# Attention and FFN kernel on one core: first q and k loads on one queue, the first GpSimd load behind the spin, and another order of the first 340 operations

## Chip, cores and metric

The kernel runs on one core of a Trainium2 chip. The metric is the device time of one execution in microseconds; before the change the median of three runs is 364.25 us (363.78 to 365.21).

## What is computed

Batch B=8, H=12 heads, sequence S=448, head size D=64. Attention without softmax: the scores are scaled, cut at zero, squared, and multiplied with v. Its result, 3584 rows of 768, goes through an FFN with exact GELU. Inputs and output are float32.

```
scores = scale * np.matmul(q, k.transpose(0, 1, 3, 2))    # scale = 1/sqrt(64)
attn = np.maximum(scores, 0.0) ** 2 / S
x = np.matmul(attn, v)              # then heads side by side: (3584, 768)
h = x @ w_in                        # 768 -> 2048
g = 0.5 * h * (1.0 + erf(h * inv_sqrt2))
return g @ w_out                    # 2048 -> 768
```

## The kernel before

The work goes batch by batch, and within a batch in three groups of four heads. For one group, k and q are brought into the layout in which the contraction (D) lies along partitions; TensorE makes scores in steps (`add_steps`, L819: four matmuls, two heads at a time, one block of keys), each into one of three PSUM banks "w"; ACT or DVE cuts them at zero and scales them (relu, L831 on ACT, L833 on DVE); DVE squares them (L841); TensorE multiplies with v (`add_av`, L881); ACT or DVE copies the result as `xT` (the copies of L566 on DVE and L568 on ACT). The FFN works on `xT`: matmuls with w_in (L940), GELU on ACT (L950), then w_out; later batches use a form with sums of operands (L1092, L1281). FFN matmuls of one batch are mixed with attention of later ones.

For batches 0 and 1 the change of layout is done on TensorE, with an identity matrix `ident` as the second operand: k in `add_tk` (L676, L680), q in `add_tq` (L708, L715), into one of two PSUM buffers "f", from which DVE or ACT copies them to `kT` and `qT`. For later batches the DMA queue of SyncE (SP) transposes.

Loads that turn float32 into bfloat16 on the way are issued by GpSimd (POOL): k (L605), q (L514), v (L623), w_in (L529 to L531), w_out (L535). At most eight are under way: a later one waits for the landing of the one eight ahead of it. Only the first group's k and the first half of its q take another way, at the start: they are loaded as float32 into `q32` and `k32` by SP and ACT (L1439 to L1442), k in a first part of four key blocks (256 KB) and a rest of three (192 KB), q's half being 224 KB; ACT casts q to `nq` and the rest of k to `nk` (L568), DVE casts the first part of k (L566). The second half of that group's q (112 KB in bfloat16's columns 128 of 256 a row) comes through GpSimd.

While the first loads are on their way, TensorE runs ten matmuls of 512 columns on a tile of zeros (L1461, the spin). `ident` is set to zero by DVE (L1445), and GpSimd puts the ones on its diagonal (affine_select, L1448).

The order is written out by hand: `ORDER` is a string of 1468 words, each an engine's letter (P TensorE, A ACT, D DVE, G GpSimd, S SyncE) with the number of an operation, and the scheduler emits the operations in that order. Each engine works through its own queue in order; an instruction that waits holds up all behind it on its engine. In the table P27 is the transposing of the second half of the first group's q (eight transposes), G7 its load; G0 and G1 are the loads of the second group's k and q; D13, A10 and A16 the casts of the first k part, the first q half and the rest of k; G1468 is the affine_select. The scheduler's numbers for when the first loads land are used to estimate times and don't change an order that is written out.

Of the kernel before, what the change touches and what calls it, by code (L numbers as in the profile page):

```python
# [12 lines left out]
B, H, S, D = 8, 12, 448, 64  # L13
KC = 112
NC = S // KC
HC = NC // 2
HS = S // 2
KB = 64
NK = S // KB
# [22 lines left out]
NB = 512  # L42
# [45 lines left out]
SPIN = 10  # L88
# [8 lines left out]
A58 A102 D91 P129 P143 D94 D100 D103 P158 A144 A159 P104 A105 A106 G132 P146 D130 D147 D128 S213
P229 P170 P182 D183 G9 A230 P155 A171 D154 A156 P227 G114 P140 A141 D160 P194 P164 D165 A195 A228
P237 P149 P173 G131 P200 G134 P239 A238 P241 D145 A150 A201 A174 D148 D157 A240 P176 A177 D151 D142
D172 P161 D184 A162 A242 D166 P179 P167 P235 P233 D175 D178 D163 D180 P197 P206 G118 A168 A236 D169  # L100
A198 D181 A234 P185 D207 P203 A186 P188 P231 A187 A232 P243 D214 G221 P247 A244 S212 A248 D202 D204
P249 A250 P245 D189 A246 P257 P272 D199 D205 P191 P269 D192 A258 A273 A270 G117 P255 A256 D190 G138
P251 P266 D196 D193 S215 P275 A276 D208 S216 D267 A252 P209 A210 P281 P284 A211 P356 P340 A282 G133
D217 D285 P290 P305 P308 D291 D292 A357 P342 G137 G260 A341 A309 P344 G259 G136 D283 D306 A343 A345
P253 P299 P293 P278 D268 D286 D279 D280 D271 A254 P350 A351 P352 A353 P358 A359 S219 D220 P346 A347
D300 D301 D277 P362 A363 P366 P364 P302 D294 S218 D274 D295 P317 D303 P287 A318 A367 P329 P296 A365
A288 D310 A330 D304 D307 D289 D297 P360 A361 P354 A355 G222 P370 G223 G225 G261 P326 S389 D390 P314
A315 P332 D333 A327 P372 P323 S388 P320 G262 A321 G264 G224 A371 D380 D298 P311 P439 S392 D324 D328
D322 D381 P430 P368 D383 A373 D384 A312 D334 D313 D316 A369 P348 A349 P338 A431 A339 P377 D382 A378
D385 A440 P411 S395 A412 G139 P445 D387 G226 A446 D325 D441 D407 G399 D386 P436 D331 D408 P433 P374  # L110
A375 A437 A434 P415 G263 G403 D393 D409 S391 P413 P457 P460 A461 S379 D319 D414 P335 P442 D458 P451
A336 A416 A452 P417 P419 D459 A443 A337 S394 D432 D396 D447 D418 D410 P454 P463 D420 P427 A428 P421
P423 P475 G265 D435 D553 D438 A455 A464 D429 P466 D444 G398 P448 D424 A476 D467 D422 G400 D456 G405
P478 P484 P521 G404 G397 G402 A485 D479 D462 D468 D477 A449 P525 D465 D453 A522 S532 A450 P469 P481
D533 A526 P487 A488 A470 P511 A482 S531 P517 P493 D471 P490 S538 P472 D494 D495 D483 S535 A491 A512
G540 D473 G401 A518 D474 P606 P594 P529 A607 A595 P519 A530 P597 P591 P603 A520 P527 D551 D552 D489
A604 D480 D605 A528 G545 P501 A502 P513 A514 D592 D608 D598 S534 P505 A506 G542 P507 P600 D492 D593
P609 D486 P496 A610 D536 A508 A497 D601 G406 A498 P627 P630 D631 P523 A628 D602 A524 S537 S539 P615
P618 P633 P503 P509 D632 A619 G548 D611 A634 A504 D635 P515 D629 A510 D596 P499 P621 D599 A616 S376
A500 A622 P624 G541 D625 P612 A516 A613 S696 D620 P657 D614 D617 D626 P645 A658 S702 G550 P555 A646  # L120
A556 G544 D554 S426 S695 P557 P559 D697 S425 D623 P757 S699 G710 P639 P636 A758 D640 G547 P648 D558
A560 P760 D637 A761 P561 A638 P563 D641 D562 G708 D700 G705 D659 P654 A649 D650 G706 P772 P651 A773
D564 D571 A655 P565 A652 D566 D573 D572 P567 D568 P766 P754 P642 A643 A767 D656 G546 G549 S698 G709
P575 D653 D644 P577 P769 D774 D768 D647 S701 A576 A755 P778 A779 D770 D762 P660 P763 G712 P790 A764
A661 A791 P579 D578 S569 P581 D756 P787 P793 D771 D574 A580 A662 P796 A794 A797 D582 D765 D780 D792
A788 P583 S703 D759 D584 D789 P585 P808 G543 G707 S827 P802 A803 P775 P784 S829 G842 D809 P781 D586
P587 P669 S826 D795 D828 A782 D783 G837 A776 A777 D798 A785 D714 A670 P805 S830 P814 A815 D786 D806
S833 P799 P811 D810 D588 P817 S831 S570 D800 D801 D804 P667 A818 P671 A812 A668 P870 A871 D807 P867
P873 D816 D874 A868 P677 A672 P876 P820 P864 D819 A678 P691 A692 A877 P689 G711 P673 D875 D872 D821
D715 G838 S832 P891 D813 A865 D822 D892 G840 G713 P894 P823 A690 P879 D824 A895 A674 D896 P900 A880  # L130
P665 A825 D834 P663 G843 G839 D866 A901 G835 G836 G704 P882 P888 A666 D869 A664 P903 A889 A883 P683
S937 S940 A684 D893 P687 P693 P927 D717 D878 A904 S942 P897 D881 D884 A928 P885 P906 D898 A688 A694
S943 D907 P921 P679 S941 S590 A680 P685 S939 D899 G841 D905 A922 D938 P681 A686 D944 S936 P718 D902
A682 D908 S589 D716 P675 A719 D890 D929 P722 A676 D923 A886 A887 P915 P912 P1000 A916 D913 P720
A1001 D917 P964 D914 P909 A965 D721 D1002 A723 P958 D966 P924 A910 G945 P724 A959 D925 A911 D960
P952 P976 D725 P930 A953 P726 D977 A931 D926 P918 P946 D932 A919 P728 D727 A947 D734 P979 D920 P933
A980 D729 D735 P955 D948 P949 A934 P730 A956 D950 A935 D957 P961 P994 D951 P1009 A962 P738 D731 A995
D963 S733 D954 P740 A1010 D739 S732 D736 P742 D741 D737 D996 P997 A743 P988 P967 D998 A989 D1011
P985 P1006 A968 D999 P744 A986 D1007 A969 D981 P1012 P973 P970 A1013 D745 P746 D974 A971 D1008 P1003
P982 A1004 D747 P748 D1014 A983 D1005 P750 D749 D984 S752 D972 P848 D975 D987 P1015 A849 D978 D990  # L140
D1018 P991 A1016 A1017 D1026 P852 A992 D1019 A993 D1027 P1030 D1021 P1049 A1031 P1051 D1028 A1050
P1144 D1052 P1068 A1145 D844 P1034 A1069 D751 P1125 A1035 D1022 P1055 A1126 P1148 D845 P1053 D1056
A1149 P1072 D1029 A1054 P1106 A1073 D1025 P1087 A1107 D1023 P1089 A1088 P1110 D1090 P1091 A1111 D846
P1093 A1092 D1020 P850 D1094 D847 P1061 D851 P1099 D1024 A853 P1127 P1032 D1062 P1095 D1128 A1063
P1108 D1033 D1096 P856 D1109 A1098 D1100 P1036 D1242 A1101 P1131 D1037 P854 D1132 D1243 P1137 D855
P1042 D1138 P1163 D857 A1139 P1038 D1043 A1164 P860 D1039 A1044 D1244 A1041 P1102 D861 P1133 D1245
P1129 D1134 P1045 A1130 D1103 P1167 A1136 D1046 A1105 P1165 A1168 P1070 A1048 D1166 P858 P1057 A1040
D859 P1140 A1047 D1071 S862 A1135 P1169 D1058 A1097 P1146 A1104 D1141 S753 A1059 P1064 D1170 A1142
A1143 P1112 D1147 A1060 S863 P1074 D1065 D1113 P1314 A1066 A1067 D1075 P1076 A1315 P1118 D1077 P1080
D1119 A1078 P1150 A1079 D1081 A1120 P1152 D1151 A1082 P1171 D1153 P1156 D1172 A1155 P1175 A1154  # L150
D1157 A1174 P1178 A1173 D1176 A1158 P1318 D1179 A1177 P1114 A1180 D1182 P1159 A1181 D1184 P1186
D1183 D1115 P1263 A1187 D1185 P1083 A1116 D1160 A1264 P1188 A1117 D1084 A1162 A1161 A1085 P1190
A1086 D1189 P1316 A1191 P1192 D1317 P1331 D1193 P1121 A1332 P1194 D1122 A1123 A1124 P1333 D1195
P1265 D1202 P1198 D1204 D1203 P1267 D1334 P1196 D1199 D1205 D1266 P1320 D1197 P1335 D1321 S1200
P1206 S1201 P1208 A1207 P1210 D1209 P1212 A1211 P1337 D1213 P1214 D1224 D1338 P1325 D1215 P1216
D1222 D1326 D1223 P1342 D1217 P1365 D1343 P1218 S1220 A1366 P1226 A1268 D1219 A1327 D1225 S1221
A1344 P1367 D1227 A1336 P1269 A1319 D1368 P1280 D1270 P1228 A1281 P1284 D1229 P1369 A1285 P1322
A1370 P1282 D1323 P1230 D1283 P1328 A1231 P1286 D1329 P1297 D1287 P1299 A1298 P1291 D1300 P1274
D1292 P1232 D1275 A1293 A1276 P1246 D1233 P1303 A1247 P1236 D1304 P1350 D1237 P1371 P1308 P1234
D1309 A1310 P1250 D1372 P1288 D1235 A1251 P1348 S1240 D1289 P1238 P1301 A1324 D1239 P1271 A1330  # L160
S1241 P1294 A1349 D1272 A1302 P1376 D1351 A1290 P1352 D1295 A1273 P1354 D1377 A1353 P1248 A1296
# [1491 lines left out]
```

## Time and profile before

| What | us |
|---|---|
| median of three runs | 364.25 |
| the profiled execution's own time | 364.45 |
| its span, first to last instruction | 362.7 |
| first scores (L819) start | 6.65 |
| first relu (L831) starts | 7.08 |
| first FFN matmul (L940) starts | 27.00 |

The profile shows one execution, in which times are counted from the start of its span. PE is TensorE's matmuls, PEld its loading of the stationary operand, which lies beside them; DVE is VectorE, ACT is ScalarE, POOL is GpSimd, SP is SyncE. A row of the timeline has the start, the length from first start to last end of a run of like instructions, the engine, the line, what is written and read with shapes, the count, and in brackets how long the engine had been idle and what released it. The rows themselves are shown where they are used, below.

### The profile page before, as it was taken

To read this page: it belongs to the slowest core of one execution; us is meant where nothing else is said; L and a number is where in the kernel's file an instruction comes from. 1 tells how busy PE (TensorE), PEld (TensorE's weight loads), DVE (VectorE), ACT (ScalarE), POOL (GpSimd) and SP (SyncE) were. 2 spreads that over 40 slices of the span, in tenths; PEclk is the share of its full clock that TensorE was granted. 3 is DMA by queue.
4 is the path that set the end of the run, shared out by engine and by line. 5 is a ranking of instruction groups with operands and counts; after the bars stand their busy time and mean duration, and the time that the engine had idled before them with its cause. 6 is when DMAs were issued, how large, how long until landed. Compare 5 with 4: busy or idle time off the path is not lost.

```text
span 362.7 us, 7632 instructions
## 1 busy us (share of the span) xinstructions
PE 353.4 (97%) x3099; PEld 189.9 (52%) x3099; DVE 296.4 (82%) x497; ACT 211.3 (58%) x354; POOL 67.1 (19%) x102
## 2 busy tenths in 40 slices
PE   8799999999999999999999999999999999999995
PEld 4464544555544555554455555555555555555663
DVE  3999788869999878999979999998966655786552
ACT  5999665546678685777958864625740333662110
POOL 8566174110902161070000000000000000000000
PEclk9999999999999999999999999999999999999999
DMA  9999999999999999999951511000301210302223
GB/s 172 201 202 201 184 175 194 173 197 207 160 188 152 228 203 146 220 168 202 164 133 11 95 61 45 3 0 19 114 0 53 78 45 2 87 2 87 88 89 88
DMA packets 72083, 43.83 MB, mean 121 GB/s; under 512 B 36336, under 2 KB 68720, under 8 KB 72048
## 3 DMA queue, kind: packets, MB, share of 16 engines
q0 software_dynamic: 32032, 22.47, 43.7%
q1 hardware_dynamic: 39120, 20.03, 29.8%
q10 hardware_dynamic: 896, 0.85, 0.7%
q8 instruction: 24, 0.39, 0.4%
q14 instruction: 11, 0.09, 0.1%
HBM read 45.61 MB, written 11.01 MB: 156 GB/s over the span
## 4 chain that ended last, share of the span: by engine, by line
PE 87%; DVE 5%; ACT 4%; issue 1%; DMA 1%; DVEq 0%
PE pso L1281 30%; PE psh L940 20%; PE pb L1092 18%; PE ps L819 8%; PE pav L881 7%; ACT a_sq L831 4%; PE pso L1388 3%; DVE a_sq L841 2%; DVE osb L1315 1%; DMA q<-in_q_dram 1%; DVE a_sq L833 1%; DVE qT L566 1%; ACT xT L568 0%; DVE s_sb L1260 0%; PE tp L715 0%
## 5 line engine op out<-in xcount | busy, mean ns | idle before, releaser
L831 ACT ACTIVATE a_sq<-ps 128x896 bf16<-128x896 f32 x122 | 107.1, 923 | 28.7 <-PE ps L819 27.0
L841 DVE TENSOR_TENSOR a_sq<-a_sq 128x896 bf16<-128x896 bf16 x169 | 96.8, 617 | 2.2 <-ACT a_sq L831 1.8
L940 PE MATMUL psh<-xT,win_sb 128*128 128x448 bf16 x384 | 77.1, 353 | 0.0
L833 DVE TENSOR_SCALAR a_sq<-ps 128x896 bf16<-128x896 f32 (+1 forms) x47 | 50.6, 1078 | 13.1 <-PE ps L819 12.8
L1281 PEld LDWEIGHTS <-s_sb 128*128 128x128 bf16 x424 | 40.4, 98 | 29.7 <-issue 3.5
L940 PEld LDWEIGHTS <-win_sb 128*128 128x128 bf16 x384 | 35.6, 98 | 38.0 <-issue 7.4
L1123 DVE TENSOR_TENSOR part<-pb,part 128x448 f32<-128x448 f32 x80 | 46.5, 620 | 9.0 <-PE pb L1092 6.2
L819 PE MATMUL ps<-qT,kT 64*64 64x448 bf16 (+1 forms) x700 | 48.2, 350 | 2.5 <-ACT a_sq L831 2.0
L950 ACT ACTIVATE h_sb<-psh 128x448 bf16<-128x448 f32 x64 | 34.4, 548 | 19.2 <-PE psh L940 19.2
L1315 DVE TENSOR_TENSOR osb<-pso,p_sb 128x384 f32<-128x384 f32 x39 | 21.7, 555 | 23.6 <-PE pso L1281 18.1
L1281 PEld LDWEIGHTS <-h_sb 128*128 128x128 bf16 x296 | 28.2, 98 | 21.5 <-issue 3.0
L1281 PE MATMUL pso<-t_sb,s_sb 128*128 128x384 bf16 x208 | 38.1, 326 | 0.0
L1144 ACT ACTIVATE h_sb<-part 128x448 bf16<-128x448 f32 (+1 forms) x48 | 24.5, 537 | 22.8 <-DVE part L1123 22.7
L1281 PE MATMUL pso<-wout_sb,s_sb 128*128 128x384 bf16 (+1 forms) x208 | 37.7, 324 | 0.0
L881 PE MATMUL pav<-a_sq,v_sb 64*64 64x448 bf16 (+1 forms) x700 | 36.0, 342 | 0.8 <-ACT a_sq L831 0.8
L1281 PE MATMUL pso<-wout_sb,h_sb 128*128 128x384 bf16 x192 | 35.2, 326 | 0.0
L819 PEld LDWEIGHTS <-kT 64*64 64x64 bf16 x700 | 18.4, 105 | 25.9 <-issue 19.1
L1092 PEld LDWEIGHTS <-win_sb 128*128 128x128 bf16 x192 | 18.8, 98 | 16.7
L881 PEld LDWEIGHTS <-v_sb 64*64 64x64 bf16 x700 | 20.6, 107 | 12.5 <-issue 2.1
L1092 PE MATMUL pb<-xs,ws 128*128 128x448 bf16 x96 | 21.9, 352 | 0.0
L1092 PE MATMUL pb<-xT,win_sb 128*128 128x448 bf16 x96 | 21.8, 352 | 0.0
L1092 PE MATMUL pb<-xs,win_sb 128*128 128x448 bf16 x96 | 21.8, 352 | 0.0
(71 smaller groups left out, 310.7 us busy)
## 6 DMA issues: line engine op xcount, KB each, us to landing
nk<-in_k_dram POOLq DMA_DIRECT2D x23, 224.0 KB, 8.5
nq<-in_q_dram POOLq DMA_DIRECT2D x23, 224.0 KB, 9.2
v_sb<-in_v_dram POOLq DMA_DIRECT2D x4, 672.0 KB, 9.7
out_dram<-osb SPq DMA_DIRECT2D x7, 336.0 KB, 3.3
v_sb<-in_v_dram POOLq DMA_DIRECT2D x10, 224.0 KB, 7.5
out_dram<-osb SPq DMA_DIRECT2D x7, 288.0 KB, 3.4
out_dram<-osb SPq DMA_DIRECT2D x8, 240.0 KB, 2.8
win_sb<-in_moe_w_in_dram POOLq DMA_DIRECT2D x8, 192.0 KB, 9.5
```

What stands on the lines that cost most here:

```text
L819: nc.tensor.matmul(ps[64 * j : 64 * j + 64, e, x * w : x * w + w], kT[r, g, i * 128 + 64 * j : i * 128 + 64 * j + 64], moving, start=True, ...
L831: A.activation(ar, ps, AF.Relu, scale=c_att)
L833: V.tensor_scalar(ar, ps, c_att, 0.0, op0=mybir.AluOpType.mult, op1=mybir.AluOpType.max,)
L841: V.tensor_mul(box["a2"][:, :, :used], ar, ar)
L881: nc.tensor.matmul(pav[0][o2 : o2 + 64, e, :w], get_v()[r, 2 * v_slot(b, g) + e, bass.ts(i, D)], box["a2"][r, y, o : o + w], start=(i == 0 ...
L940: nc.tensor.matmul(ph[:, x * n : x * n + n], win_sb[:, kd, bass.ts(m + x, 128)], xT[b][:, kd, c], start=(kd == 0), stop=(kd == KD - 1),)
L950: A.activation(h_ring()[:, m : m + nm, o + c.start : o + c.stop], box[0][:, :S].rearrange("p (x n) -> p x n", x=nm), AF.Gelu,)
L1092: nc.tensor.matmul(ps[name][:, :S], w[:, k, bass.ts(mm, 128)], right()[:, k], start=first and k == 0, stop=k == K1 - 1, skip_group_check=n ...
L1123: V.tensor_add(get(to), ps[name][:, :S], get(other))
L1144: A.activation(to(), src()[:, n0:n1], AF.Gelu)
L1281: nc.tensor.matmul(box[bank][:, n0:n1], left()[:, kf], right()[:, kf, n0:n1], start=bool(need) and kf == 0, stop=kf == K2 - 1, skip_group_ ...
L1315: V.tensor_add(out()[:, n0:n1], box[bank][:, n0:n1], other()[:, n0:n1])
```

## The change

It has five parts. The two loads of k move from ACT's DMA queue to SP's, behind q's. The spin becomes seven matmuls of 512 columns with one of 256 ahead and one behind, the first of which writes the second half of the bank. DVE copies a column of that second half into `ident`, and sets `ident` to zero only after that, so that GpSimd's affine_select has to wait for both. In `ORDER` that affine_select comes first and G7 ahead of G0 and G1, and some 340 further words are in another order (the table's rest, from P372 on, is the same but for the place of one load). The scheduler's landing times are other numbers.

```diff
-SPIN = 10
+SPIN = 7
 ORDER = """
-D13 G0 A10 G1 G7 G4 A16 G108 G1468 P11 D12 P14 D15 P17 P29 P32 D18 P38 D39 P19 P21 A30 D20 P35
...
+G1468 D13 G7 G0 A10 G1 G4 A16 G108 P11 G2 P14 D12 A15 G3 P27 P17 G111 A28 P32 D18 A33 G107 P53 P44
...
     first = slice(0, K_CUT * D)
-    nc.scalar.dma_start(k32[:, :, first], kv_view(k, 0, 0, 1)[:, :, first])
     nc.sync.dma_start(q32, q_view(0, 0, 1, 0, HC))
+    nc.sync.dma_start(k32[:, :, first], kv_view(k, 0, 0, 1)[:, :, first])
     rest = slice(K_CUT * D, NK * D)
-    nc.scalar.dma_start(k32[:, :, rest], kv_view(k, 0, 0, 1)[:, :, rest])
+    nc.sync.dma_start(k32[:, :, rest], kv_view(k, 0, 0, 1)[:, :, rest])
     zero = const.tile([128, 128], BF16, tag="zero", name="zero")
     V.memset(zero, 0.0)
-    V.memset(ident, 0.0)
...
     spin = banks.take("spin")
-    for _ in range(SPIN):
-        wide = zero[:, :1].to_broadcast([128, NB])
-        nc.tensor.matmul(spin[:, 0], zero, wide, start=True, stop=True)
+    for n, c in enumerate((NB // 2,) + (NB,) * SPIN + (NB // 2,)):
+        wide = zero[:, :1].to_broadcast([128, c])
+        nc.tensor.matmul(spin[:, int(n == 0), :c], zero, wide, start=True, stop=True)
+    V.tensor_copy(ident[:, :1], spin[:, 1, :1])
+    V.memset(ident, 0.0)
     banks.give(spin)
...
-    o = early("ACT", lambda: by_head(nat_q(0, 0)[:, :, : HC * D]), src, 4 * HC * D, 4.95)
+    o = early("ACT", lambda: by_head(nat_q(0, 0)[:, :, : HC * D]), src, 4 * HC * D, 3.45)
...
-    for eng, i0, i1, t in (("DVE", 0, K_CUT, 5.1), ("ACT", K_CUT, NK, 5.45)):
+    for eng, i0, i1, t in (("DVE", 0, K_CUT, 4.2), ("ACT", K_CUT, NK, 4.75)):
```

In the built program the lines of the early part stand one or two lower than before (L1448 is L1446, L714 was L715).

The first rows of DVE's queue before the change (in brackets the engine or DMA queue whose semaphore is waited for):

```order
L1444 MEMSET zero 128x64
L1445 MEMSET ident 128x64
L1454 MEMSET warm 128x1
L566 CAST nk<-k_92 128x512 [waits DMAHW0_49]
L566 COPY qT<-tp 128x2x224 [waits PE_49]
L566 COPY kT<-tp 128x512 [waits PE_49]
```

The same place in the changed program:

```order
L1443 MEMSET zero 128x64
L1452 MEMSET warm 128x1
L565 CAST nk<-k_92 128x512 [waits DMAHW1_49]
L1460 CAST ident<-spin 128x1 [waits PE_49]
L1461 MEMSET ident 128x64 [waits DVE_49]
L565 COPY qT<-tp 128x2x224 [waits PE_49]
```

The memset of `ident` has moved behind the cast of k's first part, which waits for k's load, and behind the copy out of the spin bank, whose wait counts nine matmuls of PE: all of the spin.

The first rows of GpSimd's queue that do work, before:

```order
L605 DMA nk<-in_k_dram 128x2x448
L514 DMA nq<-in_q_dram 112x4x256
L514 DMA nq<-in_q_dram 112x4x128
L514 DMA nq<-in_q_dram 112x4x256 x2
L1448 ISA
L1448 AFFINE_SELECT ident<-ident 128x128 [waits DVE_49]
```

And in the changed program:

```order
L1446 ISA
L1446 AFFINE_SELECT ident<-ident 128x128 [waits DVE_49]
L513 DMA nq<-in_q_dram 112x4x128
L604 DMA nk<-in_k_dram 128x2x448
L513 DMA nq<-in_q_dram 112x4x256 x3
L622 DMA v_sb<-in_v_dram 128x2x448
```

The affine_select, which waits for DVE's memset, now stands ahead of all loads, and the load of 128 columns a row (G7, the second half of the first group's q) is the first of them; before, five loads were issued ahead of it.

TensorE's queue from the transposes of k's first part to the first scores, in the changed program (the first two of the eight pairs of L714 are shown, and the first of the three of the rest of k):

```order
L675 MATMUL tp<-ident,nk 128x128
L714 LDWEIGHTS nq [waits DMASW0_49]
L714 MATMUL tp<-ident,nq 64x112 [waits DVE_49]
L714 LDWEIGHTS nq
L714 MATMUL tp<-ident,nq 64x112
...
L675 LDWEIGHTS nk [waits Activation_49]
L675 MATMUL tp<-ident,nk 128x128 [waits Activation_49]
...
L818 LDWEIGHTS kT
L818 MATMUL ps<-qT,kT 64x224
```

Before, the rest of k was followed by scores at once:

```order
L676 LDWEIGHTS nk [waits Activation_49]
L676 MATMUL tp<-ident,nk 128x128 [waits DVE_49]
L676 LDWEIGHTS nk
L676 MATMUL tp<-ident,nk 128x128
...
L819 LDWEIGHTS kT [waits DVE_49]
L819 MATMUL ps<-qT,kT 64x224
```

Eight transposes of the second half of q, with a wait for a GpSimd DMA (DMASW0), now stand ahead of the first scores; before, they came behind several steps of scores.

More of the change, by code (lines that the diff above doesn't have):

```diff
@@ L97 @@
[L97 to L106, printed above, removed]
@@ new lines @@
+A1060 S863 P1074 D1065 D1113 P1314 A1066 A1067 D1075 P1076 A1315 P1118 D1077 P1080 D1119 A1078 P1150
+A1079 D1081 A1120 P1152 D1151 A1082 P1171 D1153 P1156 D1172 A1155 P1175 A1154 D1157 A1174 P1178
+A1173 D1176 A1158 P1318 D1179 A1177 P1114 A1180 D1182 P1159 A1181 D1184 P1186 D1183 D1115 P1263
+A1187 D1185 P1083 A1116 D1160 A1264 P1188 A1117 D1084 A1162 A1161 A1085 P1190 A1086 D1189 P1316
+A1191 P1192 D1317 P1331 D1193 P1121 A1332 P1194 D1122 A1123 A1124 P1333 D1195 P1265 D1202 P1198
+D1204 D1203 P1267 D1334 P1196 D1199 D1205 D1266 P1320 D1197 P1335 D1321 S1200 P1206 S1201 P1208
@@ new lines @@
+A1207 P1210 D1209 P1212 A1211 P1337 D1213 P1214 D1224 D1338 P1325 D1215 P1216 D1222 D1326 D1223
+P1342 D1217 P1365 D1343 P1218 S1220 A1366 P1226 A1268 D1219 A1327 D1225 S1221 A1344 P1367 D1227
+A1336 P1269 A1319 D1368 P1280 D1270 P1228 A1281 P1284 D1229 P1369 A1285 P1322 A1370 P1282 D1323
+P1230 D1283 P1328 A1231 P1286 D1329 P1297 D1287 P1299 A1298 P1291 D1300 P1274 D1292 P1232 D1275
+A1293 A1276 P1246 D1233 P1303 A1247 P1236 D1304 P1350 D1237 P1371 P1308 P1234 D1309 A1310 P1250
+D1372 P1288 D1235 A1251 P1348 S1240 D1289 P1238 P1301 A1324 D1239 P1271 A1330 S1241 P1294 A1349
@@ new lines @@
+D1272 A1302 P1376 D1351 A1290 P1352 D1295 A1273 P1354 D1377 A1353 P1248 A1296 D1355 P1305 A1378
+D1249 P1373 D1306 P1252 D1374 A1307 P1339 D1253 A1375 P1379 D1340 P1257 D1380 A1341 P1359 D1258
+A1381 P1345 D1360 A1259 P1356 D1346 A1361 P1277 D1357 A1347 P1254 D1382 A1358 P1386 D1384 D1383
+P1362 D1255 A1387 P1388 D1385 A1256 D1278 D1363 P1390 A1279 D1389 A1364 P1392 A1391 P1260 D1393
+P1394 D1404 D1261 P1396 A1262 D1395 D1402 P1311 D1403 P1398 D1397 D1312 S1400 A1313 P1406 D1399
+D1405 S1401 P1408 A1407 P1410 D1409 P1412 A1411 P1414 D1413 D1424 P1416 D1415 D1422 P1418 D1423
@@ L171 @@
+D1417 S1420 P1426 D1419 D1425 S1421 P1428 A1427 P1430 D1429 P1432 A1431 P1434 D1433 D1444 P1436
+D1435 D1442 P1438 D1443 D1437 S1440 P1446 D1439 D1445 S1441 P1448 A1447 P1450 D1449 P1452 A1451
+S1463 P1454 D1453 P1456 D1455 S1464 D1458 P1459 D1457 S1465 P1460 D1461 S1466 D1462 S1467
 """
```

124 lines of the change are left out of this document (56 added, 68 removed).

## The prediction

> **What bounds the kernel now.** First the page's busy shares, then a table of four stretches of the span, then the chain of waits and the timeline of the first 12 us. The columns of the table are the stretch, its length, busy time (instructions) of PE, PEld, DVE, ACT, POOL, then granted clock, DMA share, GB/s.
>
> ```profile
> PE 353.4 (97%) x3099; PEld 189.9 (52%) x3099; DVE 296.4 (82%) x497; ACT 211.3 (58%) x354; POOL 67.1 (19%) x102
> ...
> 4.00:7.08 3.08, 2.39 (x31) 1.26 (x29) 1.60 (x4) 1.13 (x2) 3.00 (x6) 1.00 1.33 224
> 7.08:27.00 19.92, 16.84 (x390) 11.14 (x383) 19.10 (x35) 19.82 (x29) 12.76 (x19) 1.00 1.34 201
> 27.00:77.24 50.24, 50.24 (x450) 24.75 (x446) 41.46 (x62) 32.64 (x55) 20.66 (x30) 1.00 1.30 186
> 77.24:362.70 285.46, 280.90 (x2238) 151.68 (x2234) 234.09 (x393) 156.23 (x268) 27.75 (x41) 1.00 0.61 103
> ```
>
> PE is at 97%, so the average says "PE". The stretches say more. From the first relu (7.08) to the first FFN matmul (27.00) ACT works 19.82 of 19.92 us and DVE 19.10: that stretch is as long as its relus and copies, and starts when the first scores come. From 27.00 to 77.24 PE is never idle. So time lost ahead of the first relu goes through to the end: ACT cannot catch up in its own stretch, nor PE in the next. The changed orders come together again at about 77 us; behind that the two tables differ in the place of one load.
>
> How the first relu is reached (start, length, engine, line, what; in brackets the idle time before and its releaser):
>
> ```profile
> 0.74 0.48 ACTq L1439 DMA_DIRECT2D k<-in_k_dram  x1
> 0.74 0.38 SPq L1440 DMA_DIRECT2D q<-in_q_dram  x1
> ...
> 0.90 0.11 DVE L1445 MEMSET ident<- 128x64 uint32 x1
> 0.96 0.06 DVE L1454 MEMSET warm<- 128x1 f32 x1
> ...
> 0.99 4.05 PE L1461 MATMUL spin<-zero 128*128 128x512 bf16 x10 [0.99 <-DVE zero L1444]
> 1.25 0.82 POOL L605 DMA_DIRECT2D nk<-in_k_dram  x1 [0.80 <-POOLq L1637]
> ...
> 2.06 2.83 POOL L514 DMA_DIRECT2D nq<-in_q_dram  x4
> ...
> 4.79 0.62 ACT L568 CAST nq<-q 112x512 bf16<-112x512 f32 x1 [1.53 <-DMA q<-in_q_dram]
> 4.96 0.32 POOL L1448 TENSOR_SCALAR_AFFINE_SELECT ident<-ident 128x128 bf16<-128x128 bf16 x1
> 5.04 0.52 DVE L566 CAST nk<-k 128x512 bf16<-128x512 f32 x1 [4.03 <-DMA k<-in_k_dram]
> 5.20 0.73 POOL L623 DMA_DIRECT2D v_sb<-in_v_dram  x1
> ...
> 6.65 0.74 PE L819 MATMUL ps<-qT,kT 64*64 64x224 bf16 x20
> 7.08 3.44 ACT L831 ACTIVATE a_sq<-ps 128x896 bf16<-128x896 f32 x4 [1.17 <-PE ps L819]
> ...
> 8.64 0.39 PE L715 MATMUL tp<-ident,nq 112*64 112x112 bf16 x8
> ```
>
> Today the path is q and k landing (4.79, 5.04), cast, transpose, scores, relu. The second half of group 0's q, a GpSimd load, is transposed only at 8.64, behind the first scores: off the path.
>
> **The change part by part.**
>
> *The hold.* In the changed DVE queue the copy out of the spin bank stands behind the cast of k's first part, and waits for the ninth and last spin matmul; the memset of ident follows it, then POOL's affine_select, and all of GpSimd's loads stand behind that. In words: no GpSimd load is issued until k has landed and been cast. Today the first one is issued at 1.25. When does it go now? Both hardware loads' bytes are visible in the DMA rate (slices of 0.125 us from 1.0):
>
> ```profile
> GB/s 0 0 0 0 0 0 41 16 12 20 4 8 16 172 274 352 348 393 373 365 369 385 385 355 345 344 344 327 288 228 201 222 201 201 215 194 219 176 174 197
> ```
>
> From about 2.6 the rate is some 370. q and k's first part are 480 KB, 1.3 us at that rate: they can't be in before 3.9, and need not be later than now, 5.04; I take 4.6. Cast 0.52, copy 0.06 (as the warm memset), memset 0.11, two steps between instructions of some 0.05: 5.4. The loads behind affine_select went out 0.24 after its start (4.96, 5.20): issue at about 5.65. The floor is set by the spin, eight times 0.43 from 0.99, which ends near 4.4: with 0.3 to drain, 5.2; the ceiling, with k at 5.04, is 6.1.
>
> *What waits for it.* Third in PE's new order are the eight transposes of group 0's second half of q (P27). They wait for that GpSimd load, and every score matmul stands behind them. How long a GpSimd load takes to land:
>
> ```profile
> L605 POOL DMA_DIRECT2D nk<-in_k_dram x1: 820/820/820, 1.2 to 1.2; - x1
> ...
> DMA to landing us min/median/max: 5.0/5.0/5.0
> ...
> L514 POOL DMA_DIRECT2D nq<-in_q_dram x1: 706/706/706, 116.0 to 116.0; - x1
> ...
> DMA to landing us min/median/max: 4.5/4.5/4.5
> ```
>
> The first of the kernel took 5.0, and a later one of 224 KB, with little beside it, 4.5. This one is 112 KB; at 200 GB/s the missing half is 0.56 us: 3.9 to 4.4, say 4.1. P27 starts at 5.65 + 4.1 = 9.75 (bounds 5.2 + 3.9 = 9.1 and 6.1 + 4.4 = 10.5). The eight transposes take 0.39 by the row of 8.64, scores to relu 0.43 (6.65 to 7.08), and the last transposes of k come between: 0.9. First relu at 10.65 instead of 7.08: **+3.6** (2.9 to 4.3).
>
> *Shorter spin* (8 x 512 columns for 10) and ident's later place: PE is free 0.86 earlier and waits for P27 anyway: nothing. ident is late by less than P27.
>
> *k's loads behind q on SP's queue*: ACT saves two issues (0.48 and 0.49) ahead of its table load, which has slack until 4.79; k is issued 0.38 later. Both lie inside the 3.9 to 5.04 above. The Trainium skill, "DMA: Bandwidth & Descriptors", section "Issuing engines are not separate DMA queues", says that transfers of all issuing engines share the same 16 DMA engines, so that a second issuer saves only issue time. By it the one queue costs k 0.38 where the bytes weren't the limit; no run yet shows one queue alone.
>
> *The moved work.* ACT and the first FFN matmul:
>
> ```profile
> L831 ACT ACTIVATE a_sq<-ps 128x896 bf16<-128x896 f32 x21 | 18.0, 944 | 1.3 <-PE ps L819 1.2
> L568 ACT CAST xT<-pav 128x448 bf16<-128x448 f32 x4 | 1.9, 536 | 0.0
> L568 ACT CAST xT<-pav 128x224 bf16<-128x224 f32 x4 | 1.4, 389 | 0.0
> L831 ACT ACTIVATE a_sq<-ps 128x448 bf16<-128x448 f32 x1 | 0.6, 649 | 0.0
> ```
>
> That is 21.9 us of partly overlapping work. The new order has 20 full relus, two T copies, two full and one half cast ahead of that matmul. A T copy of 128x896 isn't seen on ACT today: between 0.62, what DVE takes, and 0.94, a relu of that shape; I take the relu's share, 18.0 / 21 = 0.86. 22 x 0.86 + 0.95 + 0.35 = 20.2. In the stretch's 19.92 that is at best -1.5. But the casts go to DVE, itself at 19.10, and two nearly full engines that feed each other leave gaps. I take **-0.6** (0 to -1.5). One step of scores less is done ahead of the first FFN matmul, and PE has to fit it in later: 16 matmuls, four steps, take 0.97 below, so **+0.2**.
>
> ```profile
> 11.80 0.97 PE L819 MATMUL ps<-qT,kT 64*64 64x448 bf16 x16
> ...
> 27.00 1.31 PE L940 MATMUL psh<-xT,win_sb 128*128 128x448 bf16 x6
> ...
> 41.86 6.98 PE L940 MATMUL psh<-xT,win_sb 128*128 128x448 bf16 x36
> ...
> 52.24 1.49 PE L881 MATMUL pav<-a_sq,v_sb 64*64 64x448 bf16 x28
> ```
>
> *Later loads.* GpSimd's whole stream starts 4.4 later, PE's work 3.2. Two loads have little slack:
>
> ```profile
> L531 POOL DMA_DIRECT2D win_sb<-in_moe_w_in_dram x1: 630/630/630, 35.0 to 35.0; - x1
> ...
> DMA to landing us min/median/max: 11.5/11.5/11.5
> ...
> L623 POOL DMA_DIRECT2D v_sb<-in_v_dram x1: 727/727/727, 44.8 to 44.8; - x1
> ...
> DMA to landing us min/median/max: 6.3/6.3/6.3
> ```
>
> The last w_in chunk lands at 46.5; its first user is the sixth group of six L940 in the row of 41.86, at 41.86 + 30 x 0.194 = 47.7: 1.2 us. v lands at 51.1 for the matmuls at 52.24: 1.1. If the loads move by the full 4.4, both are just covered; if some move by 0.7, one issue, more, one stalls PE, by up to about that and a tenth. Two such: from 0 to 0.8; I take **+0.2**, since most transfers of today ran only from 4.5 on, and move by less than their issue.
>
> Sum: 3.6 - 0.6 + 0.2 + 0.2 = +3.4. On the profiled execution's 364.45 (its span is 362.7) that is 367.85; that execution is 0.2 above the median of the runs shown, so **367.7**.
>
> **The rivals.**
>
> *The hold is short, so the change costs nothing* (other side). If the copy waited only for the first, short spin matmul and ran ahead of the cast, the memset would be done at about 1.8, the load issued at 2.1, P27 would start at 6.0 to 6.5, the first relu at about 7.1, and with -0.6 + 0.2 the time is 364.0 (at best 363.2). It decides in favour when P27 starts before some 6.3. Against it: the copy's row in the built program, behind the cast and with a wait on PE's last spin matmul. 0.06.
>
> *The load lands quickly.* Alone, 112 KB could run at the 390 GB/s that the hardware loads reached: 0.29 where 224 KB at 200 took 1.12, so 4.5 - 0.83 = 3.7 to land. With the floor's issue at 5.2, P27 is at 8.9, the first relu at 9.8, +2.7; with moved work at -1.2 and the step's 0.2 that is 366.0 beside the median. For: DMA is empty then. Against: the bytes of the first GpSimd loads came late today too. 0.12.
>
> *The clock falls back.*
>
> ```profile
> 3.96 0.15 PEld L1461 LDWEIGHTS <-zero 128*128 128x128 bf16 x1 [0.28 <-issue]
> 4.38 0.15 PEld L1461 LDWEIGHTS <-zero 128*128 128x128 bf16 x1 [0.28 <-issue]
> ...
> 5.46 0.37 PE L708 MATMUL tp<-ident,nq 112*128 112x112 bf16 x4 [0.42 <-ACT nq L568]
> ```
>
> Spin matmuls of 512 columns follow each other at 0.43, an L940 of 448 at 0.194: PE starts at half pace, and still has it at 4.38, 3.4 us into the spin. The new spin ends there, PE does 0.8 us of transposes and is idle for 3 us. It may then run P27 and the first scores at half pace. The first relu comes 0.4 to 0.6 later, and PE, 16.84 of 19.92 busy, falls behind for some microseconds: +1.0, 368.7. 0.16. "TensorE: Matmul & The Clock Gate" in the Trainium skill, section "What's actually happening", states half rate as the default, and a window of about 3.4 us that decides both ways; by it the shorter spin and the gap both speak for this rival's 368.7, where a clock that stays up gives 367.7. The trace agrees on the half pace (0.43 for 512 columns), though the clock column of the profile reads 1.00 from 4.00 on, and shows no gap like the new one.
>
> *More loads stall*, two or more where I took a quarter of one: +0.8 more, 368.5. 0.09.
>
> **How the numbers follow.** Forecast 0.57 (366.7 to 368.6, its terms' bounds not all at one end), the rivals 0.06, 0.12, 0.16, 0.09. The range leaves out the short hold, the lower third of the quick landing, and about 0.06 at the top where clock and loads add up: 366.2 to 369.4. A measurement of this kernel can tell about 0.5% from no change, so the bounds are 362.4 and 366.1. Faster: 0.02. Same: the rest of the short hold and the lower part of the quick landing, 0.08. Slower: 0.90.
>
> **What the new profile would show.** GpSimd's first load issued at 5.2 to 6.1, right behind DVE's cast, copy and memset; PE idle some 3 us, ended by "DMA nq" ahead of eight L714 matmuls; first relu at 10 to 11.4; first FFN matmul near 30, and no idle PE behind it but for a load. Wrong would be a first load before 3, score matmuls ahead of those eight, or a first relu as late as I say and an FFN start that isn't: then ACT's stretch had slack that I didn't see.

## The result, and the profile after

The changed kernel takes 369.25 us, the median of six runs (367.93 to 370.32); the kernel before 364.18 (363.78 to 365.21, six runs). The ratio is 1.0135, 95% interval 1.0107 to 1.0163: slower by 5.07 us. I forecast 367.7 in a range of 366.2 to 369.4, slower with a chance of 0.90. The time lies in the range, 0.15 under its top, and above the 366.7 to 368.6 that the forecast gave without its rivals. The working's sum was +3.4 on the profiled execution; the profiled executions differ by 4.15 (368.60 against 364.45), the medians by 5.07. A few executions of other kernels below, and of the kernel before beside them, took 1.6% to several times longer than the rest; medians and ratios leave them out.

The page's line of busy shares, then the table by stretches, cut at the new first relu (10.29), first FFN matmul (31.09) and the place where the two orders meet again (81.81); columns as in the prediction:

```profile
span 366.8 us, 7624 instructions
...
PE 355.3 (97%) x3098; PEld 190.1 (52%) x3098; DVE 294.9 (80%) x496; ACT 215.3 (59%) x356; POOL 66.2 (18%) x102
...
7.08:10.29 3.21, 1.59 (x23) 0.92 (x27) 0.36 (x1) 0.66 (x3) 3.21 (x5) 1.00 1.19 138
10.29:31.09 20.80, 17.56 (x379) 10.87 (x377) 19.63 (x37) 19.85 (x26) 13.60 (x20) 1.00 1.30 193
31.09:81.81 50.72, 50.72 (x454) 24.36 (x451) 41.80 (x63) 37.16 (x59) 20.33 (x30) 1.00 1.32 186
```

The first relu is 3.21 late, the first FFN matmul 4.09 (31.09 against 27.00), the meeting point 4.57 (81.81 against 77.24). From the first FFN matmul to the meeting point PE has no idle time, as before. Behind the meeting point 0.2 is added up to the last matmul, and the last stores then land 0.7 sooner than before, so that the span grows by 4.1.

The timeline of the same execution up to the first relu:

```profile
3.67 0.62 ACT L567 CAST nq<-q 112x512 bf16<-112x512 f32 x1 [1.43 <-DMA q<-in_q_dram]
...
4.51 0.43 DVE L565 CAST nk<-k 128x512 bf16<-128x512 f32 x1 [3.57 <-DMA k<-in_k_dram]
4.86 0.15 DVE L1460 CAST ident<-spin 128x1 bf16<-128x1 f32 x1
...
5.09 0.11 DVE L1461 MEMSET ident<- 128x64 uint32 x1
5.28 0.29 POOL L1446 TENSOR_SCALAR_AFFINE_SELECT ident<-ident 128x128 bf16<-128x128 bf16 x1 [4.83 <-DVE ident L1461]
5.52 0.85 POOL L513 DMA_DIRECT2D nq<-in_q_dram  x1
...
5.95 0.63 PE L675 MATMUL tp<-ident,nk 128*128 128x128 bf16 x4
...
8.70 0.58 PE L714 MATMUL tp<-ident,nq 112*64 112x112 bf16 x8 [2.12 <-DMA nq<-in_q_dram]
...
10.29 1.73 ACT L830 ACTIVATE a_sq<-ps 128x896 bf16<-128x896 f32 x2 [0.43 <-PE ps L818]
```

Read from the top: q and k do land sooner (casts at 3.67 and 4.51; before, 4.79 and 5.04). Then the row of steps of the hold, cast, copy, memset, affine_select, and the first GpSimd load at 5.52 where it was 1.25. PE waits for that load until 8.70. And PE runs at half pace: four transposes of k take 0.63, where they took 0.39. The clock column doesn't show this: it reads 1.00 in the row of 7.08 to 10.29, as it did from 4.00 on before, with spin matmuls still 0.43 apart at 4.38; the pace is read from durations here.

### The profile page after: what moved, and what is told of

The parts are those of the page before. It is cut to its first block, busy times and chain, and to the rows that moved or that the text cites. A ratio compares the mean times of both kernels' runs of the same rounds, so it can differ in the third digit from the quotient of the medians.

```text
span 366.8 us, 7624 instructions
## 1 busy us (share of the span) xinstructions
PE 355.3 (97%) x3098; PEld 190.1 (52%) x3098; DVE 294.9 (80%) x496; ACT 215.3 (59%) x356; POOL 66.2 (18%) x102
## 4 chain that ended last, share of the span: by engine, by line
PE 86%; DVE 5%; DMA 3%; ACT 2%; POOL 1%; issue 1%; SPq 0%; DVEq 0%
PE pso L1280 30%; PE psh L939 20%; PE pb L1091 17%; PE ps L818 8%; PE pav L880 7%; PE pso L1387 3%; DMA nk<-in_k_dram 2%; DVE a_sq L840 2%; ACT a_sq L830 2%; DVE osb L1314 1%; DMA k<-in_k_dram 1%; DVE a_sq L832 1%; POOL nq L513 1%; DVE qT L565 1%; PE tp L679 0%
## 5 line engine op out<-in xcount | busy, mean ns | idle before, releaser
L832 DVE TENSOR_SCALAR a_sq<-ps 128x896 bf16<-128x896 f32 (+1 forms) x46 | 48.9, 1067 | 17.4 <-PE ps L818 17.1
L1122 DVE TENSOR_TENSOR part<-pb,part 128x448 f32<-128x448 f32 x80 | 46.5, 619 | 9.0 <-PE pb L1091 6.2
L1143 ACT ACTIVATE h_sb<-part 128x448 bf16<-128x448 f32 (+1 forms) x48 | 24.5, 537 | 22.8 <-DVE part L1122 22.7
L1091 PE MATMUL pb<-xs,ws 128*128 128x448 bf16 x96 | 21.9, 352 | 0.0
```

The lines of the kernel that those rows point to most:

```text
L832: V.tensor_scalar(ar, ps, c_att, 0.0, op0=mybir.AluOpType.mult, op1=mybir.AluOpType.max,)
L1091: nc.tensor.matmul(ps[name][:, :S], w[:, k, bass.ts(mm, 128)], right()[:, k], start=first and k == 0, stop=k == K1 - 1, skip_group_check=n ...
L1122: V.tensor_add(get(to), ps[name][:, :S], get(other))
L1143: A.activation(to(), src()[:, n0:n1], AF.Gelu)
```

## Experiments

Three questions: how much is the hold; is it the wait of P27 ahead of the first relu, as I forecast, or something else that the hold delays; and what do the other parts cost by themselves. "Over before" is the difference of the medians on the same chip, the interval that of the ratio; the last three columns are from each profiled execution. The kernels ran on several chips, so kernels are compared by "over before". The chunk of w_in is the fourth and last; its landing is issue and time to landing added, as in the prediction, and shows how late the stream of GpSimd loads runs.

| Kernel | us | over before | ratio, 95% | first GpSimd load | first relu | last w_in chunk lands |
|---|---|---|---|---|---|---|
| before | 364.18 | | | 1.25 | 7.08 | 46.5 |
| changed | 369.25 | 5.07 | 1.0107 to 1.0163 | 5.52 | 10.29 | 51.0 |
| e1_no_hold | 365.57 | 1.18 | 1.0022 to 1.0061 | 1.47 | 8.11 | 47.2 |
| e7_short_hold | 366.28 | 1.62 | 1.0032 to 1.0075 | 2.10 | 7.49 | 48.3 |
| e11_half_hold | 367.22 | 2.56 | 1.0038 to 1.0098 | 3.80 | 8.05 | 49.0 |
| e12_only_first_load_early | 368.41 | 4.14 | 1.0071 to 1.0153 | 1.29, next 5.34 | 8.04 | 49.8 |
| e2_hold_more_spin | 369.48 | 5.09 | 1.0120 to 1.0169 | 5.52 | 10.02 | 52.5 |
| e8_hold_pe_busy | 368.84 | 4.55 | 1.0102 to 1.0144 | | | |
| e3_short_spin_only | 364.81 | 0.42 | 0.9989 to 1.0026 | 1.24 | 7.56 | 46.7 |
| e6_no_hold_long_spin | 365.12 | 0.73 | 1.0011 to 1.0046 | 1.46 | 8.32 | 47.4 |
| e4_new_order_only | 365.10 | 0.81 | 1.0014 to 1.0056 | 1.47 | 7.90 | 47.7 |
| e5_one_queue_only | 368.17 | 3.88 | 1.0093 to 1.0128 | 1.24 | 9.85 | 47.6 |
| e9_hold_old_order | 371.38 | 7.09 | 1.0179 to 1.0218 | 6.15 | 7.86 | 51.9 |
| e10_old_order_short_hold | 368.39 | 3.73 | 1.0074 to 1.0146 | 3.17 | 7.08 | 51.6 |

### The hold

**e1_no_hold.** The changed kernel with `ident` cleared at the start:

```diff
     V.memset(zero, 0.0)
+    V.memset(ident, 0.0)
...
-    V.tensor_copy(ident[:, :1], spin[:, 1, :1])
-    V.memset(ident, 0.0)
```

> The changed kernel with ident set to zero at the start again and without the copy out of the spin bank, so that GpSimd's first load goes out near 1.3 instead of 5.52; queue of the loads, short spin and new order stay. If the hold is the main cost: P27 starts near 6 to 6.5 instead of 8.70, the first relu near 7.3 to 7.8 (still at half pace) instead of 10.29, and of the 5 us lost 3 to 4 come back: 364.5 to 366.2. If the new order is what costs: the first relu comes early too, but the first FFN matmul is still 3 us or more late, and the time stays above 367.

365.57, or 1.18 over the kernel before: 3.9 of the 5.1 us come back. The first relu, at 8.11, is 0.3 later than I allowed. The hold is the main cost, and the order by itself is not what keeps the time above 367.

**e7_short_hold** and **e11_half_hold.** The spin matmuls are split over two banks; the copy reads the first, so that it waits only for the matmuls written there (one of 256 columns, or that and four of 512), and stands ahead of the cast of k:

```diff
-    spin = banks.take("spin")
+    head = banks.take("head")
...
-    V.tensor_copy(ident[:, :1], spin[:, 1, :1])
+    V.tensor_copy(ident[:, :1], head[:, 0, :1])
     V.memset(ident, 0.0)
+    spin = banks.take("spin")
...
```

> The changed kernel, but the first spin matmul writes a bank of its own, so that DVE's copy waits for that one alone and stands ahead of the cast of k. GpSimd's first load goes out near 2.1 (5.52 in the changed kernel, 1.47 without a hold). If the loss grows with the lateness of the loads: within 0.5 of the run without the hold, 365.2 to 366.0. If a short hold also lets q and k land unhindered, as a hold is good for: rest of k before 5.6, first relu before 7.6, and the time at or under the kernel before's.

> As the run with the short hold, with five spin matmuls ahead of the copy: the first load near 3.8 to 4.0. If the loss is in proportion to the lateness of the first load (3.7 us of time for 4.05 us of lateness between the run without the hold and the changed kernel): near 367.6. If loads issued before some 4.5 wait for the hardware loads' bytes anyway, so that an issue up to there is free: the second half of q lands at 6.6 to 7.2, and the time is within 0.6 of the short hold.

366.28 and 367.22, or 1.62 and 2.56 over the kernel before: between the run without a hold and the changed kernel. Both first expectations were near (e7 is 0.3 over its upper end, e11 0.4 under its figure), and neither kernel is faster than the one before. One thing did not fit the forecast's mechanism: e7 has its first relu 0.6 sooner than e1 and is no faster (1.62 over against 1.18, with overlapping intervals).

**e12_only_first_load_early.** The experiment that tells the two readings apart. Only the load that P27 waits for goes out early; the rest of the stream stays held:

```diff
-G1468 D13 G7 G0 A10 G1 G4 A16 G108 P11 G2 P14 D12 A15 G3 P27 P17 G111 A28 P32 D18 A33 G107 P53 P44
+D13 G7 G1468 G0 A10 G1 G4 A16 G108 P11 G2 P14 D12 A15 G3 P27 P17 G111 A28 P32 D18 A33 G107 P53 P44
```

> The changed kernel with G7, the load that P27 waits for, issued ahead of the held affine_select, near 1.25; all other GpSimd loads are held as before and begin near 5.5, with one fewer ahead of the second group's k (5.5 instead of 6.36). So the first relu comes without the wait, near 7.2 to 7.7 instead of 10.29, while the stream of loads behind it starts late. If the wait for P27 is what costs, as I forecast: about 3 us come back, 366.0 to 366.6. If the late start of the whole stream is what costs: only the 0.85 by which the stream starts sooner comes back, 368.0 to 368.8, and the first FFN matmul stays near 30 to 30.5.

368.41. Its timeline (first loads, P27, first relu, the second group's k, and the first FFN matmul):

```profile
1.29 0.84 POOL L513 DMA_DIRECT2D nq<-in_q_dram  x1 [0.84 <-POOLq L1637]
...
5.34 0.71 POOL L604 DMA_DIRECT2D nk<-in_k_dram  x1
...
6.28 0.39 PE L714 MATMUL tp<-ident,nq 112*64 112x112 bf16 x8 [0.26 <-DVE qT L565]
...
8.04 1.73 ACT L830 ACTIVATE a_sq<-ps 128x896 bf16<-128x896 f32 x2 [0.65 <-PE ps L818]
...
9.39 0.96 PE L679 MATMUL tp<-ident,nk 128*64 128x128 bf16 x14 [0.69 <-DMA nk<-in_k_dram]
...
30.76 1.31 PE L939 MATMUL psh<-xT,win_sb 128*128 128x448 bf16 x6
```

P27 no longer waits for a load, and the first relu is 2.25 sooner than in the changed kernel. The first FFN matmul is 0.33 sooner, the time over the kernel before 0.9 less. Had the wait for P27 been the cost, 3 us should have come back; the interval leaves at least 2.6 us over the kernel before, where that reading gave 1.7 to 2.3. The 0.9 is what I had expected of the sooner start of the other loads alone (5.34 for 6.36). So freeing the wait for P27 gives back little by itself. Three kernels have their first relu at 8.04 to 8.11, and their times lie 1.18 (e1), 2.56 (e11) and 4.14 (e12) over the kernel before: in the order of their streams, not of their relus.

Two further rows show the stream of the changed kernel and of e12 (issue of the last w_in chunk, and its time to landing). In the changed kernel it lands at 38.9 + 12.1 = 51.0, 4.5 later than before:

```profile
L530 POOL DMA_DIRECT2D win_sb<-in_moe_w_in_dram x1: 632/632/632, 38.9 to 38.9; - x1
...
DMA to landing us min/median/max: 12.1/12.1/12.1
```

In e12 at 49.8:

```profile
L530 POOL DMA_DIRECT2D win_sb<-in_moe_w_in_dram x1: 630/630/630, 37.9 to 37.9; - x1
...
DMA to landing us min/median/max: 11.9/11.9/11.9
```

The 4.27 by which the first load is late is still there, as 4.5, 33 us on. The stream doesn't catch up: each load goes out only when the one eight ahead of it has landed. Where it holds up the changed kernel is shown by a row of its chain of waits, which runs through GpSimd's issues and this load, and not through P27 or the first relu; and by its list of waits between 8 and 31 us:

```profile
9.88 8.15 DMA nk<-in_k_dram
```

```profile
PE ps L818 <- ACT a_sq L830: 1.9, 6, 0.4
ACT a_sq L830 <- PE ps L818: 1.4, 3, 0.5
...
PE tp L679 <- DMA nk<-in_k_dram: 0.8, 1, 0.8
```

The third group's k, issued at 9.88 behind six others, lands at 18.03, and PE waits 0.8 for it. Before, the same load was issued at 5.90 and landed 6.7 later, at 12.6, 0.9 ahead of its transposes. The load's issue and landing before, then the transposes before and in the changed kernel:

```profile
L605 POOL DMA_DIRECT2D nk<-in_k_dram x1: 730/730/730, 5.9 to 5.9; - x1
...
DMA to landing us min/median/max: 6.7/6.7/6.7
```

```profile
13.52 0.58 PE L680 MATMUL tp<-ident,nk 128*64 128x128 bf16 x14
```

```profile
18.07 0.58 PE L679 MATMUL tp<-ident,nk 128*64 128x128 bf16 x14 [0.81 <-DMA nk<-in_k_dram]
```

So a slack of 0.9 met a landing 5.4 later. ACT, the engine that should have been full, waits three times for scores, the first time ahead of the first relu; from the first relu to the first FFN matmul it is idle for 0.95 of 20.80 us, before for 0.10 of 19.92.

When PE comes to these transposes goes with the rest of the way. In the traces of all the kernels in the table but e8, the first FFN matmul starts 13.0 to 13.9 us behind them. In the five that differ only in the hold they start at 15.02 (e1), 16.24 (e11), 16.96 (e7), 17.50 (e12) and 18.07 (changed), and the profiled executions' times have the same order: 364.77, 366.53, 366.84, 368.47, 368.60.

What brings PE there late isn't always the same. In the changed kernel and in e11 PE waits for the load itself (0.8 and 1.0 us). In e7 and e12 the load had landed, at 14.9 and 16.65, and PE came 2.0 and 0.85 later, having run at half clock from 7.6 and 7.07 on. The four windows of e12 (the clock is the third number from the right):

```profile
3.65:7.07 3.42, 1.57 (x21) 1.09 (x19) 1.00 (x4) 1.72 (x4) 1.97 (x4) 1.00 0.73 98
7.07:10.48 3.41, 2.72 (x45) 1.60 (x48) 1.69 (x4) 2.05 (x3) 3.41 (x6) 0.50 1.12 145
10.48:13.89 3.41, 3.03 (x56) 2.13 (x52) 3.00 (x6) 2.92 (x4) 2.43 (x4) 0.50 1.28 163
13.89:17.30 3.41, 3.41 (x64) 2.57 (x60) 2.96 (x7) 2.15 (x3) 1.92 (x4) 0.50 1.26 202
```

For e12 the late load alone leaves PE at most 0.85 to gain from a full clock, an estimate from these two times. How much of e12's and e7's loss is the clock's and how much the loads' no run separates.

Nor is the first relu without weight: in e5, below, it is 2.8 late with the stream on time, and the kernel is 3.9 slower. The hold makes both late at once, and the later of the two sets PE's way on.

### The pace of PE

**e2_hold_more_spin.** The changed kernel with more spin behind the copy:

```diff
     banks.give(spin)
+    more = banks.take("more")
+    for _ in range(3):
+        wide = zero[:, :1].to_broadcast([128, NB])
+        nc.tensor.matmul(more[:, 0], zero, wide, start=True, stop=True)
+    banks.give(more)
```

> The changed kernel with three more spin matmuls of 512 columns behind the copy, in another bank: the hold is as long, but PE is busy until near 5.9. If the shorter spin is why PE stayed at half pace (the transposes of k 0.107 apart instead of 0.055): the pace doubles before 6 and holds until P27, the first relu comes 0.5 to 0.7 after P27 sooner, near 9.7, and the time is 0.4 to 1.0 below the changed kernel's. If the pace falls back in the wait for P27 whatever came before: no change of the first relu. If the pace does not reach the end: first relu near 9.7, and the time within 0.3 of the changed kernel.

369.48: no gain. The first relu, at 10.02, is 0.27 sooner than in the changed kernel. Three stretches of its profile, of one window of the granted clock each:

```profile
5.90:9.30 3.40, 0.98 (x18) 0.61 (x15) 0.39 (x1) 0.79 (x2) 3.40 (x6) 0.97 0.71 79
9.30:12.70 3.40, 3.22 (x56) 1.94 (x56) 2.45 (x5) 2.38 (x4) 3.40 (x6) 0.53 1.18 143
12.70:16.10 3.40, 2.46 (x62) 1.48 (x62) 3.35 (x7) 3.40 (x5) 1.46 (x3) 1.00 1.29 189
```

The clock (the third number from the right) is full while PE waits for P27, at 0.98 us of work in 3.40, and falls to half for the next 3.4 us, when the scores come. So the pace falls back because of the wait, whatever the spin was. The Trainium skill, "TensorE: Matmul & The Clock Gate", section "What's actually happening", states such windows of about 3.4 us, and half rate behind an idle one; the trace agrees on the length and shows that a window in which PE works 29% of the time is idle enough.

**e8_hold_pe_busy.** That, and matmuls on zeros in the wait (the new operation shifts affine_select's number by one):

```diff
-G1468 D13 G7 G0 A10 G1 G4 A16 G108 P11 G2 P14 D12 A15 G3 P27 P17 G111 A28 P32 D18 A33 G107 P53 P44
+G1469 D13 G7 G0 A10 G1 G4 A16 G108 P11 G2 P14 D12 A15 G3 Z3584 P27 P17 G111 A28 P32 D18 A33 G107 P53 P44
```

> The changed kernel with three more spin matmuls, and seven matmuls of 512 columns on zeros ahead of P27, so that PE is busy for most of the wait for its load. The hold is as long. If the idle wait is why PE falls back to half pace: P27 near 8.7 as before, scores and transposes behind it at full pace (k's transposes 0.055 apart), first relu near 9.5, first FFN matmul 0.5 to 1.5 sooner than 31.1, and the time 0.5 to 1.2 below the changed kernel (368.0 to 368.8). If the pace costs nothing in the end: within 0.3 of it.

368.84, or 4.55 over the kernel before, against 5.07 for the changed kernel and 5.09 for e2: 0.5 less, and the intervals overlap. That lies between the two expectations and settles nothing. Its profiled execution took 465.42 and isn't used, so whether PE held its pace isn't shown.

**e3_short_spin_only** sets `SPIN = 7` in the kernel before; **e6_no_hold_long_spin** sets `SPIN = 10` in e1.

> The kernel before with seven spin matmuls instead of ten, nothing else. If the spin's length decides the pace: the first transposes and scores run at half pace (transposes of k 0.107 apart) for 2 to 5 us from 5.46 on, the first relu comes 0.3 to 0.6 later, and the time is 0.4 to 1.2 above the kernel before. If a spin of 3 us is enough, or the pace has cover: within 0.3 of it.

> As the run without the hold, and with ten full spin matmuls and the two halves. What is left of the change is k's loads on one queue with q's, GpSimd's affine_select first, and the new order. If hold and pace together are the loss: within 0.6 of the kernel before, on either side. If the new order costs something by itself: 1 us or more above it.

e3 ran at half pace until 9.8 in its profiled execution (seven transposes of k took 1.16), its first relu was 0.48 late, and its time is 0.42 over the kernel before, with no change inside the interval. e6 is 0.45 under e1, again inside the intervals, and its 0.73 over the kernel before falls between its two expectations. All three pairs (e8 and e2, e3 and the kernel before, e1 and e6) point the same way, 0.4 to 0.5; none settles it alone. They price the half pace as these kernels have it, not the three windows of e7 and e12.

### The other parts, in the program before

**e4_new_order_only** puts the new `ORDER` into the kernel before.

> The kernel before with the new order alone: affine_select ahead of the loads, G7 first, the 340 operations in their new places; k's loads on ACT's queue, ten spin matmuls, no hold. G7 is issued near 1.5 and lands near 6.5. If the new order loses by itself, because its scores wait for the second half of q and the rest of k: first relu at 7.6 to 8.3, time 0.5 to 1.5 above the kernel before. If it is as good with its loads in time: within 0.4 of it.

0.81 over, with an interval from 0.5 to 2.0: the first relu at 7.90 waits for the second half of q and the rest of k. Without the hold the new order is a small loss by itself.

**e5_one_queue_only** moves k's two loads behind q's on SP's queue:

```diff
-    nc.scalar.dma_start(k32[:, :, first], kv_view(k, 0, 0, 1)[:, :, first])
     nc.sync.dma_start(q32, q_view(0, 0, 1, 0, HC))
+    nc.sync.dma_start(k32[:, :, first], kv_view(k, 0, 0, 1)[:, :, first])
...
-    nc.scalar.dma_start(k32[:, :, rest], kv_view(k, 0, 0, 1)[:, :, rest])
+    nc.sync.dma_start(k32[:, :, rest], kv_view(k, 0, 0, 1)[:, :, rest])
```

> The kernel before with k's two loads behind q's on SP's queue, nothing else. q and k's first part should land sooner (near 4.0 and 4.5, as in the run without the hold), the rest of k later (near 6.1 where it was 5.4). If the rest of k then sets the first scores: first relu 0.4 to 0.8 later and up to 0.6 more time. If not, since ident is ready only at 5.28 anyway: within 0.3.

3.88 over, six times what I allowed. Its timeline:

```profile
1.70 0.47 SPq L1442 DMA_DIRECT2D k<-in_k_dram  x1
...
8.40 0.51 ACT L568 CAST nk<-k 128x384 bf16<-128x384 f32 x1 [3.87 <-DMA k<-in_k_dram]
8.96 0.34 PE L676 MATMUL tp<-ident,nk 128*128 128x128 bf16 x3 [2.81 <-ACT nk L568]
```

The third load in SP's row takes 6.7 us from issue to its cast; on ACT's queue the same load, issued 0.45 sooner, was cast at 5.40, 3.0 sooner. PE waits 2.81 for it. So "in a row" alone loses while GpSimd's loads run beside it. The rule of the Trainium skill that the prediction weighed ("DMA: Bandwidth & Descriptors", section "Issuing engines are not separate DMA queues": a second issuing engine saves only issue time) is not what this run shows.

**e9_hold_old_order** has the hold and affine_select ahead of the loads, with the old order, k on ACT's queue and ten spin matmuls.

```diff
-D13 G0 A10 G1 G7 G4 A16 G108 G1468 P11 D12 P14 D15 P17 P29 P32 D18 P38 D39 P19 P21 A30 D20 P35
+G1468 D13 G0 A10 G1 G7 G4 A16 G108 P11 D12 P14 D15 P17 P29 P32 D18 P38 D39 P19 P21 A30 D20 P35
...
-    V.memset(ident, 0.0)
...
+    V.tensor_copy(ident[:, :1], spin[:, 0, :1])
+    V.memset(ident, 0.0)
```

> The kernel before with the hold alone: affine_select ahead of the loads, ident cleared behind a copy out of the spin bank; old order otherwise, k on ACT's queue. GpSimd's first load (the second group's k) goes out near 5.8 to 6.1 instead of 1.25. If the lateness of the loads is the loss in whichever order: the first relu stays near 7.0, but the transposes of the second group's k, at 7.31 today, wait until 9.5 to 10.5, ACT idles there, and the time is 2 to 3.5 above the kernel before. If only the place of P27 ahead of all scores is the loss: within 0.7 of it.

7.09 over, the slowest of all and twice the most that I allowed, with a first relu at 7.86:

```profile
7.86 1.73 ACT L831 ACTIVATE a_sq<-ps 128x896 bf16<-128x896 f32 x2 [2.10 <-PE ps L819]
...
10.31 0.96 PE L680 MATMUL tp<-ident,nk 128*64 128x128 bf16 x14 [2.16 <-DMA nk<-in_k_dram]
...
13.03 0.96 PE L715 MATMUL tp<-ident,nq 112*64 112x112 bf16 x16 [1.76 <-DMA nq<-in_q_dram]
...
14.56 0.92 ACT L831 ACTIVATE a_sq<-ps 128x896 bf16<-128x896 f32 x1 [4.98 <-PE ps L819]
```

The old order asks for the second group's k and q early; held, they arrive at 10.3 and 13.0, and ACT stands still for 4.98. So the place of P27 in the new order is not what makes the hold costly. The changed kernel, whose order works first on what the short G7 brings, loses 2 us less; its hold also ends 0.63 sooner (5.52 against 6.15), so that the 2 us aren't the order's alone.

**e10_old_order_short_hold.** As e5, with affine_select first and a hold until the third of eight spin matmuls (`SPIN = 8`, three of them in the bank that the copy reads).

> The kernel before with k's loads behind q's on SP's queue, affine_select ahead of the GpSimd loads and a hold until the third of eight spin matmuls: first GpSimd load near 3.2. Old order otherwise. If the short hold keeps the DMA engines free for q and k: rest of k lands near 5.1 to 5.4 (8.4 on one queue without a hold), ident is early, the first relu comes near 6.2 to 6.6, and unless the second group's k is then late (needed near 6.8, landing near 6.9 to 7.3) the time is 0.2 to 0.8 below the kernel before. If the second group's loads are what counts: 0.5 to 2 above it.

3.73 over, again more than I allowed. The rest of k does come by 5.55 (8.40 in e5), but the first relu is at 7.08, no sooner than before, and the stream is 5 us late at the last chunk of w_in. No version tried beats the kernel before.

## Why the prediction was right, and which step was off

- **The hold's end.** Forecast 5.65 for the first GpSimd load, measured 5.52, by the steps as listed (k's cast at 4.51, copy, memset, affine_select at 5.28). Right.
- **The landing.** Forecast 4.1 after issue, measured 3.1, and P27 at 8.70 instead of 9.75. That is the mechanism of the rival "the load lands quickly", which priced 3.7: with no hardware load beside it this half-size load was quicker than any GpSimd load in the trace of before (4.5 at least).
- **From P27 to the first relu.** Forecast 0.9, measured 1.59, at half pace. That is the rival "the clock falls back" in its effect and place, though here PE had not yet left half pace; its price of +1.0 is twice what the pairs above give. The two misses partly cancel, which is luck: first relu +3.21 for +3.6.
- **The moved work: the step that failed.** I took -0.6 between first relu and first FFN matmul, since ACT has less to do; it was +0.88 (20.80 us against 19.92). The rows of ACT's groups do sum to less (20 relus, three T copies of 0.91 where I had two of 0.86, three casts: 20.7 against 21.9), but its busy time is the same, 19.85 and 19.82, because the work overlaps less; and it is idle 0.85 longer, waiting for scores. Behind the failed size stands a wrong reading: that the stretch is as long as its relus and begins with the first one, so that only the first relu's time counts. e12 refutes it: its first relu is 2.25 sooner, and the stretch behind it is 22.7 us long. In the changed kernel PE waits inside the stretch for the third group's k, which lands at 18.03. I had the stream's 4.4 in the prediction, but let it act only on two loads at 47 to 52 us, where it still had about 1 us of cover. The load to look at had 0.9 of slack, at 13.52.
- **One step of scores and later loads.** Forecast +0.4 together, measured +0.48 from the first FFN matmul to the meeting point. The sum is right, the parts are not: PE has no idle time there, so that the loads' 0.2 didn't come, and the 0.48 is longer work.
- **The sum.** That +3.4 came near the traces' +4.15 is in part luck as well. The first relu's delay, by far its largest term, came nearly as forecast, but e12, with a first relu only 0.96 late, loses almost as much.
- **Profile and median.** The changed kernel's six runs spread over 2.4 us, those of before over 1.4, and the profiled one is 0.65 under its median; +5.07 is therefore more than the trace explains. In e2's profiled execution, which took 371.57, PE waited 1.1 for a transpose of k and 0.7 for v behind the first FFN matmul. Such waits, the rival "more loads stall", are absent from the trace of the changed kernel. That they make up the rest in its slower runs fits, but wasn't seen.
- **The short hold** didn't happen: the copy stood where the built program had it. e7, which makes it happen, is 1.62 over the kernel before, so that the 364.0 that I gave this rival was wrong too (it was also counted from the profiled 364.45, where the other rivals start from the median).

What the change could have brought is there as well: q and k are cast 1.1 and 0.5 sooner. Nothing was waiting for them alone.

## What to carry to other kernels

Before holding a queue of loads, look at the slack of every load behind it: where each load waits for an earlier landing, a late start of 4 us was still 4 us late 33 us on, and the first consumer with less slack than that pays for it. To find out which wait sets the end, free the first one alone; here freeing the most visible wait (PE, 2.1 us for P27) brought 0.9 of 5.1 us. And a part that only works together with another, as the one queue with the hold, is to be priced in both settings.

## What the runs showed of the hardware that was not expected

- One 192 KB load, third in SP's row, with eight GpSimd loads issued before it was in, took 6.7 us from issue to cast (e5); with GpSimd held it was cast at 5.05, 3.4 after its issue at 1.70 (the changed kernel).
- A GpSimd load of 112 KB landed 3.1 us after issue when no hardware load was under way (the changed kernel), and 5.2 with the hardware loads beside it (e1).
- Over a wait of 2.4 us, with PE at 0.98 us of work in 3.40, the granted clock fell to half for one window of 3.4 us, behind a spin that had brought it to full (e2).
- Once at half, the clock stayed there in e12 through a window of 3.41 us in which PE was busy for 2.72 and one in which it was busy for 3.03; behind one with PE busy throughout it was full again.
